# A blocked delta-rule kernel with a PReLU feed-forward: the first batch of 32-token blocks inverted to 16 tokens on VectorE and completed by 32x32 products on TensorE

## The chip, the cores and the metric

The kernel runs on one core of a Trainium2 chip. The metric is the device time of one execution in microseconds (us). Before the change, three runs took 712.58, 713.39 and 716.21 us; the median is 713.39 us.

## What is computed

There are two parts. The first is a delta rule over 4 batches x 8 heads, 768 tokens, 48 dimensions for each head. The second is a feed-forward block over the 3072 tokens (384 to 2048 to 384) with a learned slope for negative values. Cut to what matters:

```python
k_n = k / (norm(k) + 1e-6)
for t in range(S):                              # S = 768, state: 48 x 48 for each batch and head
    y[t] = q[t] @ state
    v_old = state.T @ k_n[t]
    state = state + beta[t] * outer(k_n[t], v[t] - v_old)
x = y as (3072, 384)
h = x @ w_in                                    # 384 x 2048, given as float64
g = maximum(h, 0) + alpha * minimum(h, 0)
out = g @ w_out                                 # 2048 x 384, given as float64
```

The recurrence is evaluated in chunks of 64 tokens. Within a chunk the updates depend on each other through a unit triangular 64x64 matrix made of the weighted products of the keys; the kernel needs its inverse.

## The kernel before

**Tiling.** One step is one chunk of 64 tokens of two batches (`t` = 0, 1 on partitions 0-63 and 64-127) and their 8 heads; there are N = 24 steps. Each 64x64 triangle is cut into two 32x32 diagonal blocks and the block between them (`right`). Four steps (NJ = 4) form a batch of blocks: 4 steps x 8 heads x 4 quadrants of 32 partitions, so that after a transpose VectorE holds one 32x32 block on each partition, as 128 x (32 x 32) elements (`block`).

**Inversion of the blocks.** `grams` (L372) makes the products of the keys on TensorE and puts the weighted diagonal blocks in `same` and the ones between in `right`. `turn_in` (L437) turns `same` into `block` by four transposes. `eliminate` (L444) masks the block, sets its diagonal to one, and does 30 steps `j`, each of one product and one sum over j x (31 - j) elements (L456, L462), each needing the one before. Then it writes the inverses back in both orientations, `turned` and `inverse`, by four transposes each. It yields after each piece: `WHOLE` = 31 + 8 = 39 pieces.

**The chain of a step.** `placing` (L486) copies parts of `turned` and `inverse` on ScalarE to `diag` and `inv`. Part 0 is the left block of `diag`, part 1 the right one, part 2 the blocks of `inv` and two small copies of weights. `between_1` and `between_2` (L524, L539) make the 32x32 block between the two diagonal ones of the inverse by two sets of 16 products each; `solve`, `outputs`, `next_state`, `to_ffn` follow. `scale_v` (L556) scales the values with the norms of the keys; `grams(N, n)` gives the products of queries and keys, masked by four VectorE instructions for each two steps (L396).

**The weights.** They arrive as 64-bit floats, 512 KB pieces of `w_in` and 384 KB pieces of `w_out`. Each piece costs two ScalarE instructions (`begin`, L204 and L205) and three on VectorE (`finish`, L212, L216, L220), the latter in two parts separated by a `yield`. Staging space holds six pieces of `w_in`; a finished piece lets SP fetch the next one into its place.

**Order of the work.** [...] that order is written by hand. `weave` takes parts from several generators in proportion to their lengths. The stages that matter here are these:

1. `statics(0, NJ - 1)`: keys of the first four steps, up to the batch of blocks 0.
2. `busy(BUSY)` with BUSY = 34: 34 products of 128x512 on TensorE whose result nobody reads, then `begin_in(n_in)` (six pieces) on ScalarE and `eliminate(0)` on VectorE.
3. The first chunk, steps 0 and 1: `ready(0, True, 1)` and `pair(0, 1)`, woven with 8 parts of `conv_in`. They carry seven more `busy(1)` products.
4. A weave of steps 2 and 3, 26 parts of conversion, `statics(4, 7)` and `ffn_in(0)`, the first product of the feed-forward for chunk 0.
5. A weave of the last conversion parts, `ffn_in(1)`, two more `statics` steps and the first 12 pieces of `eliminate(1)` (SOON = 12).
6. `ffn_out(0, True)` (64 records of L750) woven with the other 27 pieces of `eliminate(1)`. After that the regular loop over the steps 4 to 23 begins.

PSUM space: `ps_big` rotates through three buffers of two banks, `ps_ffn` through two of one bank; `busy` uses the latter.

Of the kernel before, what the change touches and what calls it, by code (L numbers as in the profile page):

```python
# [25 lines left out]
FP32 = mybir.dt.float32  # L26
# [6 lines left out]
C = 64  # L33
HB = 32
W_IN_P = 512
BUSY = 34
EARLY = 8
FIRST = 6

# [2 lines left out]
def kernel(  # L42
# [82 lines left out]
    def load_q(n):  # L125
        if n < N:
            fetch(q, n, q_pad[n % NQ][:, :, 0:D])
# [122 lines left out]
        out=ones, in_=ones, compare_op=ALU.is_ge, fill=1.0, base=0,  # L250
        pattern=[[1, HB], [-1, HB]], channel_multiplier=0,
    )
    inside = const.tile([128, HB, HB], S8, name="inside")

    which = const.tile([128, 2], FP32, name="which")
    nc.gpsimd.memset(which, 0.0)
    for t in range(2):
        for i in range(2):
            nc.gpsimd.memset(which[64 * t + HB * i : 64 * t + HB * (i + 1), i : i + 1], 1.0)


    beta_t = const.tile([128, NCH, NB, H], FP32, name="beta_t")
# [141 lines left out]

    NJ = 4
    same, block, inverse, turned = {}, {}, {}, {}

    def gather(n):
        m, j = n // NJ, n % NJ
# [25 lines left out]
            yield  # L435

    def turn_in(m):  # L437
        block[m] = work.tile([128, HB, HB], FP32, name="block", bufs=1)
        yield from turns(
            lambda x: block[m][:, :, x].rearrange("b r c -> b c r"),  # L440
            lambda x: same[m][:, :, :, x].rearrange("r j h c -> r c (j h)"),
        )

    def eliminate(m):  # L444

        if m > 2:
            yield from turn_in(m)
        r = block[m]
        nc.vector.tensor_tensor(out=r, in0=r, in1=inside, op=ALU.mult)
        nc.vector.memset(r.rearrange("p r c -> p (r c)")[:, :: HB + 1], 1.0)  # L450
        yield
        for j in range(1, HB - 1):
            n = HB - 1 - j
            prod = work.tile([128, HB * HB // 4], FP32, name="prod", bufs=2)
            prod = prod[:, 0 : j * n].rearrange("p (c i) -> p c i", c=j)
            nc.vector.tensor_tensor(  # L456
                out=prod,
                in0=r[:, 0:j, j : j + 1].to_broadcast([128, j, n]),
                in1=r[:, j : j + 1, j + 1 : HB].to_broadcast([128, j, n]),
                op=ALU.mult,  # L460
            )
# [3 lines left out]
            yield  # L465
        turned[m] = work.tile([128, NJ * H, HB], FP32, name="turned", bufs=1)
# [9 lines left out]
    WHOLE = HB - 1 + 2 * PIECES  # L476

    def changes(n):

        return n > NJ  # L480

    def place(n, parts=(0, 1, 2)):
        for _ in placing(n, parts):
            pass

    def placing(n, parts):  # L486


        if n >= N:
            return  # L490
        m, j = n // NJ, n % NJ
        first, second = slice(0, HB), slice(HB, C)

        def put(dst, cols, src, i, rows=slice(0, 128), to=None, a=slice(0, 2)):
            heads = slice(j * H + a.start * G, j * H + a.stop * G)
            nc.scalar.mul(
                dst[n % NE][to or rows, a.start * G : a.stop * G, cols], src[m][rows, heads],
                which[rows, i : i + 1],
            )

        if 0 in parts:
            put(diag, first, turned, 0)
            yield
        if 1 in parts:
            put(diag, second, inverse, 1, a=slice(0, 1 if changes(n) else 2))
            yield
            if changes(n):
                for t in range(2):
                    put(diag, second, inverse, 1, half(t), half(1 - t), slice(1, 2))
                    yield  # L510
        if 2 in parts:
            put(inv, first, inverse, 0)
            yield
            if changes(n):
                put(inv, second, inverse, 1)
                yield
            w = stats[n][1]
# [123 lines left out]
    sums = const.tile([128, FP, 3, 128], FP32, name="sums")  # L641
    more = const.tile([128, FP // 2, 3, DM // 2], FP32, name="more")
    FAST = 2

    def act_of(c, i):
        if c != 1:
# [226 lines left out]
    def busy(n):  # L873

        if n > 0:
            p = ps_ffn()
            for _ in range(n):
                nc.tensor.matmul(p, ident, k_t[NJ - 1].rearrange("p g i -> p (g i)"))  # L878

    def pair(n, filler=0):  # L880

        both = (n, n + 1)
        for i in both:
            through_state(i)
        yield
        for i in both:
            solve(i)
            busy(filler)
            yield
        for i in both:  # L890
            outputs(i)
            next_state(i)
            load_late(i + 2)
            load_v(i + 3)
            busy(filler)
            yield
        for i in both:
            to_ffn(i)
        yield

    READY = 5

    def ready(n, turned=False, filler=0):

        both = (n, n + 1)
        for i in both:
            place(i, (0,))
            if not turned:
                flips(N, i)
                load_q(i + 2)  # L910
        yield
        for i in both:
            between_1(i)
        busy(filler)
        yield
        for x in (1, 2):
            for i in both:
                place(i, (x,))
        for i in both:
            grams(N, i)  # L920
        yield
        for i in both:
            between_2(i)
            scale_v(i)
            busy(filler)
            yield

    def statics(first, last):
        if first > 0:
# [38 lines left out]
    def chain(*gens):  # L968
        for g in gens:
            yield from g  # L970
# [12 lines left out]
    for _ in statics(0, NJ - 1):  # L983
        pass
    nc.scalar.copy(inside, ones)
    load_late(1)
    load_v(2)
    for i in range(2):
        scale_v(i)

    slopes()
    for i in range(2):
        flips(N, i)
    for i in range(2):
        load_q(i + 2)
    nc.scalar.mul(minus, above, -1.0)
    zeros()

    busy(BUSY)
    begin_in(n_in)  # L1000
    for _ in eliminate(0):
        pass
    n = 8
    weave(
        (chain(ready(0, True, 1), pair(0, 1)), READY + PAIR), (part(conv_in, n), n)
    )
# [49 lines left out]
    tail = feed_forward()  # L1056
    for n in range(NJ, N):

        gens = [(attention(n), SHARES), (placing(n + 1, (1, 2)), SHARES * PLACING)]
# [51 lines left out]
```

## Time and profile before

| what | value |
|---|---|
| median of three runs | 713.39 us |
| profiled execution, its own time | 714.12 us |
| its span, first to last instruction | 712.3 us |
| mean granted TensorE clock | 0.994 |
| TensorE busy | 683.1 us (96%) |
| VectorE busy | 476.5 us (67%) |
| ScalarE busy | 251.2 us (35%) |
| GpSimd busy | 18.5 us (3%) |
| read from and written to memory | 31.56 MB, 4.72 MB |

The profile is of one execution. Times in it are counted from the first instruction. PE is TensorE's matmul, PEld its weight load, DVE VectorE, ACT ScalarE, POOL GpSimd, SP the engine that issues most transfers. A matmul on 32-bit floats appears as two records. `x64` behind a group is its number of records. Busy time includes the time for which a product that nobody reads runs.

### The profile page before, as it was taken

The numbers are of one execution on the slowest core, as the hardware profiler recorded it, in microseconds if no ns is written. First come the engines' busy times: TensorE is split into PE (matmuls) and PEld (weight loads), VectorE is DVE, ScalarE is ACT, GpSimd is POOL, SyncE is SP. The second block draws the span as 40 slices with busy tenths as digits, with TensorE's granted clock in tenths as the row PEclk, the third lists the DMA queues.
The fourth block names the chain that finished last, engine by engine and source line by source line (L and its number), as shares of the span: only waits on it lengthen the run. The fifth ranks groups of instructions, "written<-read, shape, count | busy, mean of one in ns | idle before, by whom it ended". The sixth has DMA issues, their size and how long they took to land.

```text
span 712.3 us, 21783 instructions
## 1 busy us (share of the span) xinstructions
PE 683.1 (96%) x9473; PEld 580.0 (81%) x9473; DVE 476.5 (67%) x1173; ACT 251.2 (35%) x596; POOL 18.5 (3%) x72
## 2 busy tenths in 40 slices
PE   5999987889999999999999999999999999999997
PEld 5457765656668898998998998898998988989997
DVE  6976889886898738868638968538967436245151
ACT  4724766433544413423433333222234124031020
POOL 3000000000000000000000000000000000000000
PEclk9999999999999999999999999999999999999999
DMA  8904944411141130130131021021111101100000
GB/s 135 227 30 99 220 140 99 130 23 34 35 81 25 35 68 13 36 66 16 34 68 36 6 54 35 8 51 35 25 35 35 35 24 35 24 12 2 23 1 22
DMA packets 110958, 37.68 MB, mean 53 GB/s; under 512 B 104160, under 2 KB 107248, under 8 KB 110864
## 3 DMA queue, kind: packets, MB, share of 16 engines
q1 hardware_dynamic: 109280, 36.01, 23.4%
q8 instruction: 74, 1.21, 0.7%
q10 hardware_dynamic: 1584, 0.30, 0.2%
q14 instruction: 20, 0.16, 0.1%
HBM read 31.56 MB, written 4.72 MB: 51 GB/s over the span
## 4 chain that ended last, share of the span: by engine, by line
PE 81%; DVE 12%; ACT 5%; issue 1%; DMA 1%; SPq 0%; DVEq 0%
PE p_ffn L709 29%; PE p_ffn L772 26%; PE p_ffn L878 5%; PE p_ffn L750 4%; PE p_big L378 3%; PE p_big L573 3%; PE p_big L345 3%; PE p_big L600 2%; PE p_big L587 2%; PE p_big L530 2%; PE p_big L545 1%; PE p_big L616 1%; DVE prod L456 1%; DVE block L462 1%; DVE act L721 1%
## 5 line engine op out<-in xcount | busy, mean ns | idle before, releaser
L709 PE MATMUL p_ffn<-xt,w_in 128*128 128x256 f32 x1152 | 269.7, 387 | 9.5 <-DVE sums L721 3.2
L709 PEld LDWEIGHTS p_ffn<-xt,w_in 128*128 128x128 f32 x1152 | 213.9, 191 | 42.8 <-ACT w_out L204 6.8
L721 DVE SCALAR_TENSOR_TENSOR act<-act,al_t,p_ffn 128x256 f32<-128x256 f32 x176 | 76.4, 476 | 72.3 <-ACT act L719 71.4
L719 ACT ACTIVATE act<-p_ffn 128x512 f32<-128x512 f32 x88 | 52.3, 594 | 117.1 <-PE p_ffn L709 116.9
L772 PE MATMUL p_ffn<-w_out,act 128*128 128x192 f32 x480 | 83.7, 328 | 0.0
L772 PEld LDWEIGHTS p_ffn<-w_out,act 128*128 128x128 f32 x480 | 78.6, 190 | 0.9
L462 DVE TENSOR_TENSOR block<-block,prod 128x30 f32<-128x30 f32 (+9 forms) x180 | 59.7, 332 | 6.2
L456 DVE TENSOR_TENSOR prod<-block 128x30 f32<-128x30 f32 (+9 forms) x180 | 58.7, 326 | 3.3
L792 DVE TENSOR_TENSOR o_sb<-u,p_ffn 128x192 f32<-128x192 f32 x40 | 13.2, 351 | 42.4 <-PE p_ffn L772 36.1
L878 PE MATMUL p_ffn<-k_t,ident 128*128 128x512 f32 x82 | 38.8, 622 | 0.0
L581 ACT COPY y<-p_big 128x384 f32<-128x384 f32 x22 | 10.5, 478 | 67.9 <-DVE r L576 67.9
L367 ACT COPY q_t<-p_big 128x512 f32<-128x512 f32 x24 | 14.0, 588 | 57.4 <-PE p_big L345 57.4
L367 ACT COPY k_t<-p_big 128x512 f32<-128x512 f32 x24 | 13.9, 580 | 55.6 <-PE p_big L345 55.5
L422 ACT COPY same<-right 32x256 f32<-32x256 f32 x40 | 16.1, 403 | 48.6 <-DVE right L387 48.3
L878 PEld LDWEIGHTS p_ffn<-k_t,ident 128*128 128x128 f32 x82 | 15.6, 199 | 17.1 <-issue 16.7
L772 PE MATMUL p_ffn<-space_out,sums 128*128 128x192 f32 x160 | 29.3, 326 | 0.0
L772 PE MATMUL p_ffn<-more,sums 128*128 128x192 f32 x160 | 29.3, 326 | 0.0
L772 PE MATMUL p_ffn<-w_out,sums 128*128 128x192 f32 x160 | 27.7, 326 | 0.0
L772 PEld LDWEIGHTS p_ffn<-space_out,sums 128*128 128x128 f32 x160 | 26.5, 190 | 0.0
L772 PEld LDWEIGHTS p_ffn<-more,sums 128*128 128x128 f32 x160 | 26.5, 190 | 0.0
L792 DVE TENSOR_TENSOR u<-u,p_ffn 128x192 f32<-128x192 f32 x20 | 7.0, 352 | 28.9 <-PE p_ffn L772 28.7
L772 PEld LDWEIGHTS p_ffn<-w_out,sums 128*128 128x128 f32 x160 | 25.8, 190 | 0.0
(131 smaller groups left out, 952.7 us busy)
## 6 DMA issues: line engine op xcount, KB each, us to landing
w_out<-in_moe_w_in_dram SPq DMA_DIRECT2D x12, 512.0 KB, 5.3
qp<-in_q_dram SPq DMA_DIRECT2D x48, 96.0 KB, 2.9
v_raw<-in_v_dram SPq DMA_DIRECT2D x48, 96.0 KB, 2.9
kl<-in_k_dram SPq DMA_DIRECT2D x96, 48.0 KB, 2.4
out_dram<-o_sb SPq DMA_DIRECT2D x96, 48.0 KB, 1.6
space_out<-in_moe_w_out_dram SPq DMA_DIRECT2D x11, 384.0 KB, 4.2
ke<-in_k_dram SPq DMA_DIRECT2D x43, 96.0 KB, 3.6
w_out<-in_moe_w_out_dram SPq DMA_DIRECT2D x5, 384.0 KB, 3.0
```

The lines of the kernel that those rows point to most:

```text
L345: nc.tensor.transpose(p[:, g * 128 : (g + 1) * 128], src[:, 2 * g : 2 * g + 2].rearrange("p h d -> p (h d)"), ident,)
L367: nc.scalar.copy(dst.rearrange("p g i -> p (g i)"), src)
L378: nc.tensor.matmul(p[half(t ^ a if w else t), a, w, g], k_t[n][dims(a), g, half(t)], rhs[n][dims(a), g, half(t)],)
L456: nc.vector.tensor_tensor(out=prod, in0=r[:, 0:j, j : j + 1].to_broadcast([128, j, n]), in1=r[:, j : j + 1, j + 1 : HB].to_broadcast([128, ...
L462: nc.vector.tensor_tensor(out=r[:, 0:j, j + 1 : HB], in0=r[:, 0:j, j + 1 : HB], in1=prod, op=ALU.add)
L573: nc.tensor.matmul(p[half(t), a, w, g], x[n][dims(a), g, half(t)], state[bp][dims(a), t, g])
L709: nc.tensor.matmul(p_h[:, i], w_in[:, t, (f + i) * 128 : (f + i + 1) * 128], xt[:, t], start=(t == 0), stop=(t == KT - 1),)
L719: nc.scalar.activation(g, p_h, ACT.Relu, scale=-1.0)
L721: nc.vector.scalar_tensor_tensor(out=g[:, i], in0=g[:, i], scalar=al_t[:, f + i : f + i + 1], in1=p_h[:, i], op0=ALU.mult, op1=ALU.add,)
L750: nc.tensor.matmul(p_o[u], gs[f // 2][:, f % 2, u * 128 : (u + 1) * 128], w_out[:, f], start=(f == 0), stop=(f == FT - 1),)
L772: nc.tensor.matmul(p, x(i), w(i), start=(i == 0), stop=(i == FP - 1))
L878: nc.tensor.matmul(p, ident, k_t[NJ - 1].rearrange("p g i -> p (g i)"))
```

## The change

**Blocks.** `block` gets 32 spare elements at its end, so that one view (`own_blocks`) can address the two 16x16 diagonal blocks inside each 32x32 block. For the first batch, `eliminate_small` masks these two, sets the rest of the block to zero by two memsets and the diagonal to one, and does 14 steps over both at once, each over 2 x j x (15 - j) elements. `back`, the transposes at the end, is taken out of `eliminate` and shared. The other batches are inverted as before.

**The 16x16 blocks between.** `edges` copies the part of `same` that lies between the 16-token blocks to `edge` on ScalarE, with the rows of the other half set to zero by `first_of` (a new constant, one VectorE reduction). `cross` then completes `turned` and `inverse` for a range of blocks: 4 products of 32x32 by 32x16 for each block, a ScalarE copy to `half_way`, 2 and 4 more for each block, and three VectorE sums. It is called for the 16 blocks of steps 0 and 1 in `first_chunk`, and for the 16 blocks of steps 2 and 3 at the head of the next weave. `edge` lies in `sums` and `half_way` in `act`, which are free at that time; two GpSimd memsets clear parts of them.

**First chunk.** `ready(0, ...)` and `pair(0, ...)` woven with conversion are replaced by `first_chunk`, whose order is written out, with 6 parts of conversion instead of 8 and five `busy(1)` instead of seven. The products of queries and keys of steps 0 and 1 (`queries`) are issued ahead of `busy(BUSY)`, their masks within `first_chunk`; `scale_v` of steps 0 and 1 moves from before the elimination into `first_chunk`. The small copies of weights become part 3 of `placing` and are issued ahead for steps 0 and 1.

**Numbers.** BUSY goes from 34 to 8, `begin_in` from six pieces to four, SOON from 12 to 8.

```diff
-BUSY = 34
+BUSY = 8
...
-    inside = const.tile([128, HB, HB], S8, name="inside")
+    inside_ = const.tile([128, HB * (HB + 1)], S8, name="inside")
+    inside = inside_[:, 0 : HB * HB].rearrange("p (r c) -> p r c", c=HB)
...
+    first_of = const.tile([128, 1], FP32, name="first_of")
+    nc.vector.tensor_reduce(
+        out=first_of, in_=ident.rearrange("p (q u e) -> p u q e", u=2, e=HB // 2)[:, 0],
+        axis=mybir.AxisListType.XY, op=ALU.add,
+    )
...
+    def eliminate_small(m):
+        x = small[m]
+        nc.vector.tensor_tensor(out=x, in0=x, in1=own_blocks(inside_), op=ALU.mult)
+        nc.vector.memset(block[m][:, 0:LB, LB:HB], 0.0)
+        nc.vector.memset(block[m][:, LB:HB, 0:LB], 0.0)
+        nc.vector.memset(block[m].rearrange("p r c -> p (r c)")[:, :: HB + 1], 1.0)
+        yield
+        for j in range(1, LB - 1):
+            n = LB - 1 - j
+            prod = work.tile([128, HB * HB // 4], FP32, name="prod", bufs=2)
+            prod = prod[:, 0 : 2 * j * n].rearrange("p (s c i) -> p s c i", s=2, c=j)
+            nc.vector.tensor_tensor(
+                out=prod,
+                in0=x[:, :, 0:j, j : j + 1].to_broadcast([128, 2, j, n]),
+                in1=x[:, :, j : j + 1, j + 1 : LB].to_broadcast([128, 2, j, n]),
+                op=ALU.mult,
+            )
+            nc.vector.tensor_tensor(
+                out=x[:, :, 0:j, j + 1 : LB], in0=x[:, :, 0:j, j + 1 : LB], in1=prod, op=ALU.add
+            )
+            yield
+        yield from back(m)
+
+    def edges(m, dst):
+
+        src = same[m].rearrange("p j h c -> p (j h) c")[:, :, LB:HB]
+        nc.scalar.mul(dst[:, :, LB:HB], src, first_of)
...
+    def cross(m, bs, edge, half_way):
+
+        n = bs.stop - bs.start
+        p = ps_one()[:, 0 : n * LB].rearrange("p (b i) -> p b i", i=LB)
+        for b in range(n):
+            for i in range(4):
+                nc.tensor.matmul(
+                    p[quad(i), b], edge[quad(i), bs.start + b],
+                    turned[m][quad(i), bs.start + b, 0:LB],
+                )
+        nc.scalar.copy(half_way[:, bs, 0:LB], p)
+        yield
+        p = ps_big()[:, :, 0 : n * LB].rearrange("p w (b i) -> p w b i", i=LB)
+        for b in range(n):
+            for i in (0, 2):
+                nc.tensor.matmul(
+                    p[quad(i), 1, b], inverse[m][quad(i), bs.start + b],
+                    half_way[quad(i), bs.start + b, 0:LB],
+                )
+        for b in range(n):
+            for i in range(4):
+                nc.tensor.matmul(
+                    p[quad(i), 0, b], half_way[quad(i), bs.start + b],
+                    inverse[m][quad(i), bs.start + b, LB:HB],
+                )
+        for i in (0, 2):
+            y = turned[m][quad(i), bs, 0:LB]
+            nc.vector.tensor_tensor(out=y, in0=y, in1=p[quad(i), 1], op=ALU.add)
+        y = inverse[m][:, bs, LB:HB]
+        nc.vector.tensor_tensor(out=y, in0=y, in1=p[:, 0], op=ALU.add)
+        yield
...
+    edge, half_way = edge_space(sums, 0), edge_space(act, 3072)
+    nc.gpsimd.memset(edge[:, :, 0:LB], 0.0)
+    nc.gpsimd.memset(half_way[:, :, LB:HB], 0.0)
...
+    def first_chunk(mask, convert):
+
+        both = (0, 1)
+        middle = cross(0, slice(0, 2 * H), edge, half_way)
+        next(middle)
+        busy(1)
+        for i in both:
+            mask(i)
+        next(middle)
+        busy(1)
+        for i in both:
+            place(i, (0,))
+            scale_v(i)
+        for i in both:
+            between_1(i)
+            place(i, (1,))
+        convert(1)
+        busy(1)
+        for i in both:
+            place(i, (2,))
+            between_2(i)
+        for i in both:
+            through_state(i)
+        solve(0)
+        convert(1)
+        solve(1)
+        busy(1)
+        for i in both:
+            outputs(i)
+            next_state(i)
+            convert(1)
+            load_late(i + 2)
+            load_v(i + 3)
+        busy(1)
+        for i in both:
+            to_ffn(i)
+        convert(2)
...
     nc.scalar.copy(inside, ones)
+    edges(0, edge)
     load_late(1)
     load_v(2)
-    for i in range(2):
-        scale_v(i)
-
     slopes()
     for i in range(2):
         flips(N, i)
     for i in range(2):
         load_q(i + 2)
+    mask = queries()
     nc.scalar.mul(minus, above, -1.0)
     zeros()
+    for i in range(2):
+        place(i, (3,))
 
     busy(BUSY)
-    begin_in(n_in)
-    for _ in eliminate(0):
+    begin_in(4)
+    for _ in eliminate_small(0):
         pass
-    n = 8
-    weave(
-        (chain(ready(0, True, 1), pair(0, 1)), READY + PAIR), (part(conv_in, n), n)
-    )
+    n = 6
...
+    first_chunk(mask, convert)
     fetch_out(SPACES)
     n = PARTS_IN - n + 10
     weave(
-        (chain(ready(2), pair(2)), READY + PAIR), (chain(conv_in, part(conv_out, 10)), n),
+        (chain(cross(0, slice(2 * H, 4 * H), edge, half_way), ready(2), pair(2)),
+         CROSS + READY + PAIR),
+        (chain(conv_in, part(conv_out, 10)), n),
         (statics(NJ, 2 * NJ - 1), 2 * NJ + 1), (ffn_in(0), IN_PARTS),
     )
     fetch_out(len(stages))
-    blocks, SOON = eliminate(1), 12
+    blocks, SOON = eliminate(1), 8
```

More of the change, by code (lines that the diff above doesn't have):

```diff
@@ L406, with own_blocks @@
     same, block, inverse, turned = {}, {}, {}, {}
+    small = {}
+    LB = HB // 2
+    def own_blocks(flat):
+        x = flat.rearrange("p (s e) -> p s e", s=2)[:, :, 0 : HB * LB]
+        return x.rearrange("p s (r c) -> p s r c", c=HB)[:, :, :, 0:LB]
     def gather(n):
@@ L437, in turn_in @@
     def turn_in(m):
-        block[m] = work.tile([128, HB, HB], FP32, name="block", bufs=1)
+        flat = work.tile([128, HB * (HB + 1)], FP32, name="block", bufs=1)
+        block[m] = flat[:, 0 : HB * HB].rearrange("p (r c) -> p r c", c=HB)
+        small[m] = own_blocks(flat)
         yield from turns(
@@ L465, in eliminate, with back @@
             yield
+        yield from back(m)
+    def back(m):
+        r = block[m]
         turned[m] = work.tile([128, NJ * H, HB], FP32, name="turned", bufs=1)
@@ L476 @@
     WHOLE = HB - 1 + 2 * PIECES
+    def eliminate_small(m):
[19 more added lines that the diff above has]
+            yield
+        yield from back(m)
@@ new lines, in edges, with quad @@
+    def edges(m, dst):
+        src = same[m].rearrange("p j h c -> p (j h) c")[:, :, LB:HB]
+        nc.scalar.mul(dst[:, :, LB:HB], src, first_of)
+    def quad(i):
+        return slice(HB * i, HB * i + HB)
+    def cross(m, bs, edge, half_way):
[28 more added lines that the diff above has]
+        yield
@@ L478, in changes, with place @@
+    CROSS = 2
     def changes(n):
         return n > NJ
-    def place(n, parts=(0, 1, 2)):
+    def place(n, parts=(0, 1, 2, 3)):
         for _ in placing(n, parts):
@@ L516, in placing @@
                 yield
+        if 3 in parts:
             w = stats[n][1]
@@ L643, with edge_space @@
     FAST = 2
+    def edge_space(x, first):
+        flat = x.rearrange("p i s e -> p (i s e)")[:, first : first + NJ * H * HB]
+        return flat.rearrange("p (b i) -> p b i", i=HB)
+    edge, half_way = edge_space(sums, 0), edge_space(act, 3072)
+    nc.gpsimd.memset(edge[:, :, 0:LB], 0.0)
+    nc.gpsimd.memset(half_way[:, :, LB:HB], 0.0)
     def act_of(c, i):
@@ L878, in busy, with pair @@
                 nc.tensor.matmul(p, ident, k_t[NJ - 1].rearrange("p g i -> p (g i)"))
-    def pair(n, filler=0):
+    def pair(n):
         both = (n, n + 1)
@@ L887, in pair @@
             solve(i)
-            busy(filler)
             yield
@@ L894, in pair @@
             load_v(i + 3)
-            busy(filler)
             yield
@@ L901, with ready @@
     READY = 5
-    def ready(n, turned=False, filler=0):
+    def ready(n):
         both = (n, n + 1)
@@ L907, in ready @@
             place(i, (0,))
-            if not turned:
-                flips(N, i)
-                load_q(i + 2)
+            flips(N, i)
+            load_q(i + 2)
         yield
@@ L913, in ready @@
             between_1(i)
-        busy(filler)
         yield
-        for x in (1, 2):
+        for x in (1, 2, 3):
             for i in both:
@@ L924, in ready, with queries, mask @@
             scale_v(i)
-            busy(filler)
             yield
+    def queries():
+        p = ps_big().rearrange("p a (n g i) -> p a n g i", n=2, g=G)
+        for n in range(2):
+            for g, a, t in quarters():
+                nc.tensor.matmul(
+                    p[half(t ^ a), a, n, g], k_t[n][dims(a), g, half(t)],
+                    q_t[n][dims(a), g, half(t)],
+                )
+            a_t[n] = work.tile([128, H, C], FP32, name="a_t")
+        def mask(n):
+            for a in range(2):
+                nc.vector.tensor_tensor(
+                    out=a_t[n][:, a * G : (a + 1) * G], in0=p[:, a, n],
+                    in1=minus[:, None, :].to_broadcast([128, G, C]), op=ALU.mult,
+                )
+        return mask
+    def first_chunk(mask, convert):
[34 more added lines that the diff above has]
+        convert(2)
     def statics(first, last):
@@ L995, with convert @@
         load_q(i + 2)
+    mask = queries()
     nc.scalar.mul(minus, above, -1.0)
     zeros()
+    for i in range(2):
+        place(i, (3,))
     busy(BUSY)
-    begin_in(n_in)
-    for _ in eliminate(0):
-        pass
-    n = 8
-    weave(
-        (chain(ready(0, True, 1), pair(0, 1)), READY + PAIR), (part(conv_in, n), n)
-    )
+    begin_in(4)
+    for _ in eliminate_small(0):
+        pass
+    n = 6
+    def convert(n):
+        for _ in part(conv_in, n):
+            pass
+    first_chunk(mask, convert)
     fetch_out(SPACES)
@@ L1057 @@
     for n in range(NJ, N):
-        gens = [(attention(n), SHARES), (placing(n + 1, (1, 2)), SHARES * PLACING)]
+        gens = [(attention(n), SHARES), (placing(n + 1, (1, 2, 3)), SHARES * PLACING)]
         if n % NJ == 0 and n < N - NJ:
```

## The prediction

> **What bounds the kernel now.** I read the page first, then the busy time by stage, the chain of waits, and the instructions in order of time on VectorE and TensorE.
>
> ```profile
> span 712.3 us, 21783 instructions
> PE 683.1 (96%) x9473; PEld 580.0 (81%) x9473; DVE 476.5 (67%) x1173; ACT 251.2 (35%) x596; POOL 18.5 (3%) x72
> ```
>
> TensorE looks like the bound of everything. By stage it is not:
>
> ```profile
> 18.31:49.00 30.69, 30.69 (x71) 13.19 (x71) 27.69 (x76) 14.00 (x32) 0.00 (x0) 1.00 0.52 125
> 49.00:65.30 16.30, 16.30 (x405) 10.88 (x406) 9.47 (x20) 4.32 (x13) 0.00 (x0) 1.00 0.39 110
> 65.30:115.00 49.70, 45.15 (x784) 36.27 (x782) 40.03 (x91) 35.40 (x80) 2.36 (x8) 0.97 0.67 165
> 115.00:149.30 34.30, 25.22 (x167) 19.48 (x166) 30.86 (x84) 19.37 (x41) 2.25 (x4) 0.95 0.30 81
> 149.30:171.00 21.70, 21.65 (x100) 12.99 (x101) 18.27 (x50) 2.28 (x7) 0.60 (x2) 1.00 0.12 23
> ```
>
> Columns: stretch, length, busy PE, PEld, DVE, ACT, POOL, clock, DMA share, GB/s. In the first stretch TensorE is full, with 71 instructions. The chain says with what:
>
> ```profile
> 18.31 30.69 PE p_ffn L878 x68
> 49.00 1.99 PE p_big L530 x64
> 50.98 1.05 PE p_ffn L878 x2
> ```
>
> L878 is `busy`, products nobody reads. The useful work there is VectorE's elimination:
>
> ```profile
> 18.33 0.98 DVE L559 TENSOR_TENSOR v_raw<-v_raw,norm 128x384 f32<-128x384 f32 x2
> 19.23 1.22 DVE L449 TENSOR_TENSOR block<-block,inside 128x1024 f32<-128x1024 f32 x1
> 30.62 0.41 DVE L456 TENSOR_TENSOR prod<-block 128x240 f32<-128x240 f32 x1
> 31.50 0.41 DVE L456 TENSOR_TENSOR prod<-block 128x240 f32<-128x240 f32 x1
> 42.01 0.20 DVE L456 TENSOR_TENSOR prod<-block 128x30 f32<-128x30 f32 x1
> 42.50 1.96 DVE L434 STREAM_TRANSPOSE turned<-block 128x256 f32<-128x256 f32 x4
> 44.32 2.19 DVE L434 STREAM_TRANSPOSE inverse<-block 128x256 f32<-128x256 f32 x4
> ```
>
> It ends at 46.5, 2.5 us before the fillers let L530 start. From 18.3 to 49.0 no feed-forward work is possible; from 115 to 149 VectorE leads (90% busy); from 149 on TensorE does, with real work. So what is saved before 65.3 reaches the end, less what the middle stages take back.
>
> **What the Trainium skill says.** "TensorE: Matmul & The Clock Gate", section "What's actually happening": the array runs at half clock until a window of about 3.4 us was busy, and falls back after an idle one. The trace agrees: records of L878 begin 0.853 us apart at first, 0.429 us after about 3 us. The same page, "LDWEIGHTS (loading the stationary operand)": a load's time goes with the columns, about P/1.2 ns. "TensorEngine Tiling (Array Packing)", section "Key Properties": different tiles work in parallel. The trace agrees, by these rows:
>
> ```profile
> 48.93 2.06 PE L530 MATMUL p_big<-diag,right 64*64 64x32 f32 x64
> 51.97 1.16 PE L378 MATMUL p_big<-q_t,k_t 48*64 48x64 f32 x64
> 12.10 1.99 PE L378 MATMUL p_big<-k_t 48*64 48x64 f32 x64
> ```
>
> Each is 32 matmuls. L530 uses two tiles of the array: 62 ns for a matmul. L378 uses four: 34 ns. The third row is the second before the clock rises: 62 ns. No product of 32x32 by 32x16 is in the trace.
>
> **The elimination.** A pair L456 + L462 takes 0.88 us at 240 elements (30.62 to 31.50) and 0.49 at 30 (42.01 to 42.50): 0.43 + 0.0019 for an element. The old 30 pairs (4960 elements): 22.3 us, in the trace 22.0. The new 14 pairs hold 2 x j x (15 - j), 1120 in sum: 14 x 0.43 + 2.1 = 8.2 us. The mask covers 512 elements in place of 1024: 0.75 (half of 1.3, and a fixed part). The two memsets of 256 are not shown: between 0.1 (L450, 32 elements, 0.09) and 0.35 (an L462 of that size, 0.43) each; I take 0.25. `scale_v` no longer stands ahead, so the start is 18.3, not 19.2. Sum: 18.3 + 0.75 + 0.5 + 0.05 + 8.2 = 27.8; `turned` at 29.7, `inverse` at 31.8 (the transposes as before, 1.82 to the second set, then 2.19). The old `turned` came at 44.5.
>
> Ahead of this, at no cost: the reduction `first_of` runs while VectorE waits 4.0 us for the first keys; the POOL memsets (two of 512 elements, at most 0.95 each by the 1024 of L248) fill its 1.7 us idle ahead of L334 at 8.0 (0.2 us late at most); `edges` (about 0.6) lies in ScalarE's 2.7 us wait ahead of L284; part 3 (0.8) and four `begin` pieces (5.1, by L204 and L205) end near 30, before `half_way` needs ScalarE. `queries` takes 2 us at low clock after the q flips at 18.3, then eight fillers, about two slow, end near 28. SP's loads keep their order; those of `load_late` and `load_v` come 15 us sooner, behind transfers that ended at 33.
>
> **The products.** For 16 blocks: 64 on four tiles, then 32 on two, 64 on four. At the rows above 2.2 + 2.0 + 2.2 = 6.4 us, the upper bound. These weights have 32 columns, not 64; if the load sets the pace it is half, 3.2, the lower bound (not under nothing, it is added). I take 1.6 + 3.1 = 4.7.
>
> **The first chunk.** TensorE from `turned` on: 1.6; filler 0.86; 3.1; filler 0.86; L530 2.0; filler; L545 2.1; L587 1.2; filler; L600 and L616 2.2; filler; L629 0.66: 17.2, and about 0.4 of waits. ScalarE and VectorE fit beside it: `half_way` (0.4), masks (1.4) and sums (0.35 each) beside fillers and products; `scale_v` (0.98) sits behind the last sum and ahead of the `inv` sum, three fillers' time before solve; the conversions in front of u (0.7) and the state (1.1) delay the second u behind a filler. If that cover fails it costs about 1. So the weave begins at 29.7 + 17.6 = 47.3 instead of 65.3: **-18.0**.
>
> **The next weave.** It takes the other 16 blocks: TensorE 4.7, VectorE 1.1, ScalarE 0.4. One more piece of `w_in` on VectorE (0.4 + 0.7 + 0.7 = 1.8) and two on ScalarE (2.6). TensorE is busy 91% there, VectorE 81, ScalarE 71, each often awaiting another: **+4.0** (2 to 6.5).
>
> **SOON.** Four pieces of elimination (j = 8 to 11) leave the stage in which VectorE leads: -2.8 (4 x 0.69, from 137.83 to 147.87). In the next, VectorE ended at 168.7 and TensorE at 169.6; it now ends 3.2 later, 2.3 behind. What waits is `placing` of step 4 and its `between_2`; TensorE has L750 of the next chunk meanwhile. Some +1.3. Together **-1.5** (-3 to +0.5).
>
> **The clock.** Between the fillers' end near 28 and the first filler of the chunk near 31.3 TensorE does little: 1.7 us of nothing, 1.6 us of quarter-array products. A window there may count as idle; then one window of 3.4 us runs at half speed: **+1.7** (0 to 15). From 49 to 65 the mix of fillers and small products stayed at full clock; from 5 to 13 small products and transposes alone never raised it.
>
> **Sum.** -18.0 + 4.0 - 1.5 + 1.7 = -13.8. The profiled execution took 714.1: 700.3. The median shown lies 0.7 below it: **699.6**, I say 700 us.
>
> **Rivals.**
> *The clock stays low through the chunk* (0.14). For: the stretch 5 to 13, and that the fillers fall from 34 to 8 and from seven to five. Against: the stretch 49 to 65, where one window held only a quarter filler. Half the chain slow costs 8.6 instead of 1.7: 707. All of it: 715.
> *The middle gives it back* (0.11): the weights don't come sooner or the three engines wait for each other more. For: the DMA share there is 0.67. Against: only 1.5 us of waits on transfers from 115 to 150, none of note earlier, and the DMA rests from 34 to 48. Stage +10 instead of +4: 706.
> *The small products don't run side by side* (0.09): slower than before. If row tiles that share a bank exclude each other, or each switch drains, a product takes what one tile needs, 2 x 62 = 124 ns: 160 of them 19.8 us instead of 4.7, in the chunk and again in the weave. 700 + 2 x 15.1 = 730. It decides from (713.4 - 700) / 320 = 42 ns above my 29, at 71 ns. Against: L530 runs two row tiles into one bank at 62, half of 124.
>
> **How the numbers follow.** The forecast has 0.66. Its own ends are 695 (products at the lower bound, -3; no slow window, -1.7) and 706. The range 695 to 709 takes in the first two rivals but for their tails and leaves out the third. This kernel's measurement can tell about 0.5% from no change: below 709.8 counts as faster, above 717.0 as slower. Faster: 0.66 + 0.10 + 0.10 = 0.86. Slower: 0.09. Same: 0.05.
>
> **What would show it.** In the profile after: the elimination's pairs end near 28; the products' group begins near 30 and takes about 1.6 and 3.1; the first L709 of the weave stands near 48 (66.6 before), the last `sums`/`more` L721 before L750 14 us sooner than 149.2, and VectorE's last transpose after TensorE's last L750 of that stage. I am wrong if L878 in the chunk shows 0.85 between its two records, if the products take over 10 us, or if the stage 65 to 115 has grown by more than 7.

## The result, and the profile after

The changed kernel takes 702.66 us in the median of four runs (699.69 to 703.72; a fifth on record took 703.84) beside 713.99 for the kernel before in the same session, now with a fourth run: a ratio of 0.9836, with a 95% interval from 0.9801 to 0.9872. The forecast was 700 us with a range from 695 to 709.

The profiled execution took 699.69 us, span 697.9. That is the quickest of the four, and the difference matters below. Its page begins:

```profile
span 697.9 us, 22933 instructions
PE 668.1 (96%) x10057; PEld 578.0 (83%) x10057; DVE 467.0 (67%) x1150; ACT 251.8 (36%) x599; POOL 19.4 (3%) x74
```

TensorE lost 15.0 us of busy time (683.1 before) in spite of 584 more records: what went is fillers. The busy time by stage, cut as before (columns: stretch, length, busy PE, PEld, DVE, ACT, POOL, granted clock, DMA share, GB/s):

```profile
18.15:48.50 30.35, 27.54 (x741) 18.22 (x742) 22.71 (x65) 16.30 (x42) 0.00 (x0) 1.00 0.60 151
48.50:101.20 52.70, 48.87 (x1103) 39.68 (x1102) 44.10 (x98) 37.99 (x85) 2.54 (x8) 0.97 0.70 174
101.20:135.00 33.80, 24.98 (x167) 19.79 (x167) 29.10 (x77) 18.92 (x41) 2.20 (x4) 0.94 0.33 90
135.00:158.30 23.30, 23.30 (x100) 13.90 (x101) 21.16 (x58) 2.42 (x7) 0.51 (x2) 0.93 0.09 18
```

The clock column is not to be trusted at the start. It reads 1.00 for the first stage, before and after, although the records of the first fillers begin 0.85 us or more apart and the later ones 0.43: the traces hold no change of the clock before 21 us in the one and 22 us in the other.

The elimination and the first chunk together took 47.0 us before (18.31 to 65.3) and take 30.4 now. On VectorE, in order of time:

```profile
18.87 0.69 DVE L502 TENSOR_TENSOR block<-block,inside 128x512 f32<-128x512 f32 x1
19.57 0.27 DVE L503 MEMSET block<- 128x256 f32 x1
23.65 0.27 DVE L517 TENSOR_TENSOR block<-block,prod 128x112 f32<-128x112 f32 x1
27.62 0.21 DVE L517 TENSOR_TENSOR block<-block,prod 128x28 f32<-128x28 f32 x1
27.86 1.99 DVE L448 STREAM_TRANSPOSE turned<-block 128x256 f32<-128x256 f32 x4
29.70 2.15 DVE L448 STREAM_TRANSPOSE inverse<-block 128x256 f32<-128x256 f32 x4
```

`turned` is complete at 29.85; before it was at 44.46. TensorE, in order of time, goes on from there:

```profile
29.10 1.40 PE L537 MATMUL p_big<-turned,sums 32*32 32x16 f32 x128 [0.96 <-DVE turned L448]
30.43 1.12 PE L975 MATMUL p_ffn<-k_t,ident 128*128 128x512 f32 x2
32.00 1.12 PE L546 MATMUL p_big<-act,inverse 32*32 32x16 f32 x61 [0.45 <-DVE inverse L448]
33.03 1.49 PE L552 MATMUL p_big<-inverse,act 32*32 32x16 f32 x124
34.46 1.12 PE L975 MATMUL p_ffn<-k_t,ident 128*128 128x512 f32 x2
36.03 2.37 PE L618 MATMUL p_big<-diag,right 64*64 64x32 f32 x64 [0.45 <-ACT diag L583]
39.39 2.00 PE L633 MATMUL p_big<-diag,mid 64*64 64x32 f32 x62
47.72 0.82 PE L717 MATMUL p_big<-ident,y 128*128 128x128 f32 x6
```

L537, L546 and L552 are the 32x32 products, L975 the fillers (L878 before), L618 and L633 `between_1` and `between_2`. After L717, at 48.5, the next weave begins (65.3 before). Later markers, by start: the transposes of the second batch of blocks, 97.06 (110.91 before); the long group of L847 (L750 before), 135.00 (149.35); its first product of the next chunk, 157.79 (170.63). So 16.8 us are gained by 48.5, 13.9 by 97.1, 14.4 by 135.0 and 12.8 by 157.8. The last 1.6 us up to the end come from single stretches near 272 and 447 us in which the profiled execution of the kernel before lost time over the same instructions; near 447 TensorE rests for 0.9 us of it.

### The profile page after: what moved, and what is told of

Read it like the earlier page. It is cut to its first block, busy times and chain, and to the rows that moved or that the text cites. A ratio compares the mean times of both kernels' runs of the same rounds, so it can differ in the third digit from the quotient of the medians.

```text
span 697.9 us, 22933 instructions
## 1 busy us (share of the span) xinstructions
PE 668.1 (96%) x10057; PEld 578.0 (83%) x10057; DVE 467.0 (67%) x1150; ACT 251.8 (36%) x599; POOL 19.4 (3%) x74
## 3 DMA queue, kind: packets, MB, share of 16 engines
q8 instruction: 79, 1.29, 0.8%
## 4 chain that ended last, share of the span: by engine, by line
PE 78%; DVE 13%; ACT 4%; issue 2%; SPq 2%; DMA 1%; DVEq 0%; ACTq 0%
PE p_ffn L806 30%; PE p_ffn L869 27%; PE p_ffn L847 4%; PE p_big L661 3%; PE p_big L352 2%; PE p_big L385 2%; PE p_big L688 2%; PE p_big L675 2%; PE p_big L618 2%; PE p_big L633 2%; PE p_big L704 1%; SPq L119 1%; DVE act L818 1%; DVE block L478 1%; DVE prod L472 1%
## 5 line engine op out<-in xcount | busy, mean ns | idle before, releaser
L478 DVE TENSOR_TENSOR block<-block,prod 128x30 f32<-128x30 f32 (+9 forms) x150 | 49.7, 332 | 5.2
L472 DVE TENSOR_TENSOR prod<-block 128x30 f32<-128x30 f32 (+9 forms) x150 | 48.7, 325 | 2.3
L374 ACT COPY k_t<-p_big 128x512 f32<-128x512 f32 x24 | 13.9, 580 | 55.3 <-PE p_big L352 55.2
L847 PE MATMUL p_ffn<-w_out,act 128*128 128x384 f32 x64 | 22.6, 515 | 3.4 <-DVE more L818 2.4
L583 ACT ACTIVATE diag<-inverse,which 64x128 f32<-64x128 f32 (+2 forms) x62 | 25.4, 412 | 0.9
```

The source lines that it names most:

```text
L472: nc.vector.tensor_tensor(out=prod, in0=r[:, 0:j, j : j + 1].to_broadcast([128, j, n]), in1=r[:, j : j + 1, j + 1 : HB].to_broadcast([128, ...
L478: nc.vector.tensor_tensor(out=r[:, 0:j, j + 1 : HB], in0=r[:, 0:j, j + 1 : HB], in1=prod, op=ALU.add)
L583: nc.scalar.mul(dst[n % NE][to or rows, a.start * G : a.stop * G, cols], src[m][rows, heads], which[rows, i : i + 1],)
L847: nc.tensor.matmul(p_o[u], gs[f // 2][:, f % 2, u * 128 : (u + 1) * 128], w_out[:, f], start=(f == 0), stop=(f == FT - 1),)
```

## The experiments

Each ratio, with its 95% interval in brackets, is to the kernel before in the same session; there it had medians of 713.12, 714.93, 713.96 and 713.31 us in the four sessions. The changed kernel itself was timed in two sessions alone, so most comparisons with it are across sessions. "The chunk" below is the time from the first `turned` transpose to the first product of the next weave.

**Are the parts worth what they were said to be?** Three runs take the change apart. The first undoes SOON.

```diff
-    blocks, SOON = eliminate(1), 8
+    blocks, SOON = eliminate(1), 12
```

> The changed kernel with SOON back at 12, so that four more steps of the second batch's elimination stand in the stage where VectorE leads. My forecast gave SOON 1.5 us of the gain: this run should then be 1 to 2 us slower than the changed kernel (about 704), with the long group of L847 starting some 2.5 us later relative to the start of that stage (36.3 us long instead of 33.8) and VectorE ending with TensorE in the next. Rival, that SOON is worth nothing because that stage waits on something else: the stage is as long as in the changed kernel, time within 0.5 us of it.

Measured: 702.67 us, 0.9824 (0.9766 to 0.9882), the changed kernel to 0.01 us. That is closer than the runs can tell: these four spread from 696.53 to 703.20, and the interval is 4 us to either side. The trace says more. In its profile the stretch from the second batch's transposes to the long group of L847 is 38.9 us instead of 38.0, and the long group is shorter (139.09 to 160.37, 21.3 us, instead of 22.8):

```profile
139.09 20.23 PE L847 MATMUL p_ffn<-w_out,act 128*128 128x384 f32 x62 [2.39 <-DVE more L818]
```

In the changed kernel that row reads 21.73. SOON moves about 1 us here, not 2.8, and what comes after varies by more. The 1.5 us are the clock: the group follows a rest of 2.4 us, and in 10 of the 14 profiles of this study it starts at half speed (stage of 22.8 to 23.0 us), in four not (21.3); both lengths occur with SOON 12 and with SOON 8.

Where SOON is 8 and the group is fast, the late end of VectorE that the prediction feared does show: in the two profiles of that kind (the one with BUSY 10 and the second one with a filler between the sets, both below) `between_2` behind the group waits 0.99 and 1.05 us for `mid`, and in this one, with SOON 12, not at all. So the two sides of SOON, about 1 us each, roughly cancel. That is nearer to the rival than to my 1.5 us, though the rival's equal length of the stage does not hold.

The second cuts four fillers from the kernel before.

```diff
-BUSY = 34
+BUSY = 30
```

> The kernel before with BUSY 30 instead of 34, so that the fillers end with the elimination instead of 2.5 to 3.5 us after it. If a part of the gain was only these fillers being too long, this gives it: four times 0.86, 3.4 us, so 710.5 (0.995). If the first product of the chunk was waiting for ScalarE or VectorE anyway, nothing: 714.

Measured: 709.64 us, 0.9951 (0.9933 to 0.9969). The 3.4 us come in full (3.5 in the medians): L530 starts at 45.74 instead of 48.93, at once behind the fillers. About a third of the change's gain could be had with this one number.

The third keeps the new order of the chunk and the whole 32-token elimination, without the products:

```diff
-BUSY = 8
+BUSY = 26
...
-    for _ in eliminate_small(0):
+    for _ in eliminate(0):
...
-        middle = cross(0, slice(0, 2 * H), edge, half_way)
-        next(middle)
-        busy(1)
         for i in both:
             mask(i)
-        next(middle)
-        busy(1)
...
-        (chain(cross(0, slice(2 * H, 4 * H), edge, half_way), ready(2), pair(2)),
-         CROSS + READY + PAIR),
+        (chain(ready(2), pair(2)), READY + PAIR),
```

> The new order of the first chunk, queries ahead, six parts of conversion, SOON 8, but the whole 32-token inversion by VectorE and none of the 32x32 products, with BUSY 26 so that the fillers end with it. My theory: the elimination makes most of the gain (14.8 us later blocks) and the order little; blocks ready near 44 instead of 29.1, no products (5.5 us less in the chunk, 3 less in the weave after): weave starts near 58, total about 705 to 708. Rival, that the order and the fillers are the gain: as fast as the changed kernel, about 700 to 702.

Measured: 705.37 us, 0.9886 (0.9856 to 0.9915). This is inside what the theory said, but the theory's reason, that the order gives little, falls: the order and the fillers give 7.8 us, of which some 3.5 are the too long fillers of the kernel before, as the second run shows. The short elimination with its products gives 2.7 more in the medians, and 2.0 beside the later session of the changed kernel; ten of the eleven executions of that kernel on record are under the fastest of these four (704.37). TensorE's rows in order of time show a short chunk:

```profile
45.25 2.06 PE L618 MATMUL p_big<-diag,right 64*64 64x32 f32 x64
48.29 2.00 PE L633 MATMUL p_big<-diag,mid 64*64 64x32 f32 x62
56.31 0.82 PE L717 MATMUL p_big<-ident,y 128*128 128x128 f32 x6
```

11.7 us from L618 to the weave, where the kernel before needed 16.4 (48.93 to 65.3): four fillers fewer, of about 1.06 us from start to start, and the query products (1.0) issued ahead. Between the two profiles the inversion should be worth more: 704.3 against 697.9 in span, 6.4 us. Why the medians give it only 2.7 was the next question.

**Why is the median 3 us above the profile?** The clock was the suspect, and the fillers in the chunk its handle.

```diff
     # in first_chunk, five times
-        busy(1)
+        busy(0)
```

> The changed kernel without the five single fillers in the first chunk. If they only take TensorE's time, the chunk is 2 to 4 us shorter and the total about 699 to 701. If they hold the clock up, the chunk's products show their slow distance (L618 4 us for both instead of 2), the chunk is up to 5 us longer and the total is 703 to 707.

Measured: 701.66 us, 0.9836 (0.9805 to 0.9867), no slower than with the fillers. Yet in its profile the small products are slow: L618 takes 3.6 us for both steps and L633 3.5. The chunk pays for a low clock and saves five fillers; at 21.8 us it is 1.2 longer than in the first profile of the changed kernel.

```profile
35.86 3.62 PE L618 MATMUL p_big<-diag,right 64*64 64x32 f32 x64 [1.48 <-ACT diag L583]
39.29 3.50 PE L633 MATMUL p_big<-diag,mid 64*64 64x32 f32 x62
```

Next, the fillers ahead were made to end later and, in another run, left out:

```diff
-BUSY = 8
+BUSY = 10
```

> The changed kernel with BUSY 10 instead of 8: the fillers end 1.7 us later, near 30, and the second set of 32x32 products starts when it did, since it waits for the inverse transposes until 31.9. My theory now: in most executions the clock falls in the chunk, because TensorE rests for a microsecond and then runs only small products, and that makes the difference between the profiled 699.7 and the median 702.7. With the gap closed the clock should hold: L618 and L633 at the fast distance (2 us for each pair of steps), a chunk of 20 to 21 us, median 700 to 701. Rival, that the spread comes from elsewhere: median 702.5 to 704, or later by the two fillers.

Measured: 704.15 us, 0.9848 (0.9820 to 0.9875), where the rival had it. The theory fails in one part: the gap is closed (the fillers end where L537 begins), and the clock falls all the same. That the time goes with the clock stands:

```profile
20.14 9.78 PE L975 MATMUL p_ffn<-k_t,ident 128*128 128x512 f32 x20
29.85 1.43 PE L537 MATMUL p_big<-turned,sums 32*32 32x16 f32 x128
31.21 1.12 PE L975 MATMUL p_ffn<-k_t,ident 128*128 128x512 f32 x2
35.62 2.03 PE L975 MATMUL p_ffn<-k_t,ident 128*128 128x512 f32 x2
37.59 3.63 PE L618 MATMUL p_big<-diag,right 64*64 64x32 f32 x64
```

The filler at 31.21 is fast, the one at 35.62 takes twice as long. In the 3.3 us between them TensorE issued small products, with one gap of 0.8 us. Together these didn't hold the clock; which of the two brings it down, this run doesn't tell.

```diff
-BUSY = 8
+BUSY = 0
```

> The changed kernel with BUSY 0, so that TensorE rests during the elimination. If the clock in the chunk depends on the fillers ahead, all of the chunk runs at half clock until the single fillers or the feed-forward raise it: L537 takes about 2.7 us instead of 1.4, the single fillers 2.1 instead of 1.1, the chunk 26 to 30 us, total 708 to 712. If the products and the single fillers raise the clock themselves within a window, the chunk is 22 to 24 us and the total about 703 to 705.

Measured: 705.36 us, 0.9875 (0.9850 to 0.9900). The chunk is as the first theory said, slow from the start (27.9 us against 20.6 in the first profile of the changed kernel), but the total is as the second said, only 2.7 us above the changed kernel: had the clock usually held there, this run would have lost about 7. That fits a changed kernel that is itself slow in most executions.

The changed kernel was then profiled once more, without an edit.

> The changed kernel once more, without an edit, for a second profile of it. My theory: its profile at 699.7 was of an execution in which the clock held, and most others, about 702.7, are slow in the chunk: L618 and L633 at 3.5 us for their pair instead of 2, the chunk 24 to 26 us instead of 20.5. Rival, that the other executions lose their 3 us elsewhere: the chunk is 20 to 21 us in this profile too while its time is over 702.

Measured: 703.42 us in the median of six, 0.9842 (0.9811 to 0.9874); the profiled execution took 704.43. Its TensorE rows in the chunk, to be read beside those of the first profile:

```profile
28.75 1.62 PE L537 MATMUL p_big<-turned,sums 32*32 32x16 f32 x128
30.30 1.12 PE L975 MATMUL p_ffn<-k_t,ident 128*128 128x512 f32 x2
34.95 2.08 PE L975 MATMUL p_ffn<-k_t,ident 128*128 128x512 f32 x2
36.96 3.63 PE L618 MATMUL p_big<-diag,right 64*64 64x32 f32 x64
42.52 3.52 PE L633 MATMUL p_big<-diag,mid 64*64 64x32 f32 x62
52.36 1.12 PE L975 MATMUL p_ffn<-k_t,ident 128*128 128x512 f32 x2
```

And the same stretch by busy time, first in the profile of 699.7, then in this one:

```profile
28.00:48.40 20.40, 17.59 (x657) 13.05 (x656) 13.92 (x30) 6.63 (x15) 0.00 (x0) 1.00 0.40 84
```

```profile
28.00:48.40 20.40, 19.53 (x521) 14.51 (x520) 9.70 (x23) 5.17 (x12) 0.00 (x0) 0.65 0.28 51
```

The granted clock is 1.00 there in one and 0.65 in the other: in the second it is at half speed from 34.0 to 51.0. The chunk is 27.0 us instead of 20.6; the two executions end 4.7 us apart, since later stages give 1.7 back. This is shown: one program, two courses, and the difference lies in the chunk. It also shows why a single profile misleads: the first was taken where the clock held.

What starts the fall is not settled. In each of the eight profiles in which the clock fell in the first chunk after full-speed fillers, the 3.4 us ahead of the fall held small products and also 0.7 to 2.4 us of rest. In the first profile, where it held, such a stretch with 0.7 us of rest had a whole filler in it. So neither the rests nor the smallness of the products is shown to be enough alone.

**Can it be held?** One more filler, between the two last sets of products:

```diff
     # in cross, for the first chunk
                     half_way[quad(i), bs.start + b, 0:LB],
                 )
+        busy(1)
         for b in range(n):
             for i in range(4):
```

> The changed kernel with one more single filler, between the two last sets of 32x32 products of the first chunk, so that no stretch of small products is longer than 2 us. If small products count as rest for the clock and the filler is enough to hold it: L618 and L633 fast, chunk 21 to 22 us, median 699 to 701, at least 1.5 us under the changed kernel in the same call. If the clock falls all the same, the filler costs 0.9 to 1.7 us and the median is 703 to 705.

Measured: 698.93 us, 0.9809 (0.9772 to 0.9845); the changed kernel in the same session 703.42. In the profile all is fast, the chunk 21.2 us:

```profile
32.21 1.12 PE L976 MATMUL p_ffn<-k_t,ident 128*128 128x512 f32 x2
33.27 1.61 PE L553 MATMUL p_big<-inverse,act 32*32 32x16 f32 x128
36.37 2.06 PE L619 MATMUL p_big<-diag,right 64*64 64x32 f32 x64 [0.44 <-ACT diag L584]
39.41 2.00 PE L634 MATMUL p_big<-diag,mid 64*64 64x32 f32 x62
```

> The version with one more filler between the two last sets of products, unchanged, a second time. If the filler holds the clock in most executions, at least four of six are under 701.5 us and the median is 698 to 701, clear of the changed kernel's 702.7 and 703.4. If the first time was luck, the median is 702 to 704.

Measured: 701.50 us, 0.9827 (0.9791 to 0.9863), between what the two theories said; three of six were under 701.5. Its profile is of an execution (704.06) in which the clock fell in the middle of the first filler:

```profile
29.60 1.59 PE L976 MATMUL p_ffn<-k_t,ident 128*128 128x512 f32 x2
33.04 2.08 PE L976 MATMUL p_ffn<-k_t,ident 128*128 128x512 f32 x2
38.88 3.63 PE L619 MATMUL p_big<-diag,right 64*64 64x32 f32 x64
```

Of all twelve executions of this version eight were under 701.3 us, of eleven of the changed kernel two. The limit was set after seeing the times. So the filler seems to make the good course likelier, and it doesn't make it sure. Whether the version is truly quicker than the changed kernel the intervals, which overlap, don't settle.

A longer variant, with the sum into `turned` between the sets, BUSY 9 and a filler ahead of `solve`:

```diff
-BUSY = 8
+BUSY = 9
...
+        busy(1)
         solve(0)
```

> The filler between the sets, the sum into turned issued between them, BUSY 9 and one more filler ahead of solve: the version with the best chance to hold the clock. If it holds: chunk 21.5 to 23 us with fast products, median 699.5 to 701. If not, slower than the changed kernel by the three fillers, 704 to 706.

Measured: 702.99 us, 0.9850 (0.9816 to 0.9884). In its profile (706.65) the clock fell again, here behind a wait of 1.0 us for `diag` inside L620. No gain from the two further fillers is to be seen.

The earlier sum by itself:

```diff
         for b in range(n):
             for i in (0, 2):
-                nc.tensor.matmul(p[quad(i), 1, b], inverse[m]..., half_way...)
+                nc.tensor.matmul(x[quad(i), b], inverse[m]..., half_way...)
+        for i in (0, 2):
+            y = turned[m][quad(i), bs, 0:LB]
+            nc.vector.tensor_tensor(out=y, in0=y, in1=x[quad(i)], op=ALU.add)
+        p = ps_one()[:, 0 : n * LB]...
         for b in range(n):
             for i in range(4):
```

> The changed kernel with the sum into turned issued between the two last sets of 32x32 products, each set in a PSUM buffer of its own. In the profile of the changed kernel the sum starts at 34.6, after all products, though its own ended at 33.1; diag then waits for it and L618 for diag (0.45 us). If that wait sets the chunk, the sum starts near 33.2, L618 right behind the filler at 35.5, and the chunk is 0.5 us shorter here and as much in the next weave: 0.5 to 1 us in all, within the noise of the time. If the turned sum doesn't come sooner, nothing changes.

Measured: 701.76 us, 0.9837 (0.9811 to 0.9864). The sum does come sooner: it starts at 34.75, behind its own set and 1.7 us before the other set ends. L618 (here L619) stands right behind the filler without a wait for `diag`, but the clock had fallen in the profiled execution and the filler took 2.1 us, so the gain can't be read there. The median is within the noise: inconclusive, as small as was said.

**What does a product cost?**

```diff
     # in cross, for each of the three sets
-        for b in range(n):
+        for b in [x for x in range(n) for _ in range(2)]:
```

> The changed kernel with every 32x32 product issued twice (the second overwrites the first with the same numbers). Each product took about 23 ns in the changed kernel (3.8 us for 160). If they are on the path with that price, the chunk is 3.8 us longer, and the weave after it 2.5 to 3.8: total 709 to 710. If waits beside them (the inverse transposes, ScalarE's diag) hide a part, the total is 705 to 708. If the products keep TensorE active enough to hold the clock, the chunk is not slow in this run in spite of them.

Measured: 728.28 us, 1.0197 (1.0169 to 1.0226). None of the theories: 25.6 us more than the changed kernel for 320 products more, 80 ns each, where the first set of 64 had taken 1.4 us, 22 ns each. TensorE in order of time:

```profile
28.94 2.70 PE L537 MATMUL p_big<-turned,sums 32*32 32x16 f32 x233 [0.68 <-DVE turned L448]
34.19 0.51 PE L537 MATMUL p_big<-turned,sums 32*32 32x16 f32 x23 [2.56 <-issue]
65.42 1.40 PE L537 MATMUL p_big<-turned,sums 32*32 32x16 f32 x128 [0.86 <-issue]
69.42 1.37 PE L537 MATMUL p_big<-turned,sums 32*32 32x16 f32 x107 [2.60 <-issue]
79.62 1.55 PE L552 MATMUL p_big<-inverse,act 32*32 32x16 f32 x128 [3.00 <-issue]
83.35 1.79 PE L552 MATMUL p_big<-inverse,act 32*32 32x16 f32 x119 [2.18 <-issue]
```

While the clock is up, the products themselves run at the same pace as in the changed kernel. Between them TensorE rests for 0.9 to 3.0 us with nothing that the profile shows to wait for ("issue"), and twice in these rows exactly 128 records lie between two such rests. With their weight loads these are 256 instructions. The seven rests of 0.4 to 3.0 us in this stretch come to 13.4 us, so they are only a part of the 25.6: the clock is at half speed from 32.5 to 59.8, and again from 70.0 to 73.4 and from 80.2 to 90.5.

The page's queue for instructions moved 1.29 MB in 79 packets for 22,933 instructions in the changed kernel, and 1.38 MB in 84 for 24,213 here: 1,280 more instructions, five more packets, 256 for each. The trace has the times of these packets, which come 3.4 to 8.7 us apart in this stretch. Each of the seven rests ends 1.3 to 1.6 us after one of them has come in. So TensorE very likely rests until its next packet of instructions is there; no run here took the packets away. The changed kernel has such rests too, in its chain of waits:

```profile
49.36 0.76 issue
54.19 0.76 issue
```

They end 1.6 and 1.5 us after a packet; of two shorter ones in its first chunk, one ends 1.4 and one 2.2 us after. In the second profile of the changed kernel the rest of 0.9 us among the products ahead of the fall of the clock ends 1.6 us after one.

## Why the prediction was right, and where it was not

By the profile of 704.43 us, which is like most executions (times from the first instruction, against the profile of before):

| step | forecast | measured, clock fell | measured, clock held |
|---|---|---|---|
| weave begins (65.3 before) | -18.0, clock apart | -11.2 | -16.8 |
| the next weave | +4.0 | +1.9 | +3.0 |
| SOON, both stages | -1.5 | +1.2 | +1.0 |
| the clock | +1.7 | in the first row | in the first row |
| the rest | 0 | -1.6 | -1.6 |
| sum | -13.8 | -9.7 | -14.4 |

The rows of the measured columns are differences of the markers named above. "Held" is said of the first chunk; in the next weave each of the two profiles has 3.4 us at half speed.

- *The elimination.* Right. The pairs ended at 27.86 (27.8 said), `turned` was ready at 29.85 (29.7). The memset of 256 took 0.27 us (0.25 taken). The match to 0.1 us is partly luck: the mask began at 18.87, not 18.3, and the pairs took 7.8 us, not 8.2.
- *The products.* Right in size for those issued: L537 1.4 us (1.6 said), L546 and L552 2.5 (3.1), nearly at the lower bound. Four row tiles of one bank took 22 ns for a product. A filler's 512 columns take 0.86 us at full clock, so 16 columns one product after another would be some 27 ns by estimate, without any weight load: the tiles did run side by side, as the Trainium skill, "TensorEngine Tiling (Array Packing)", section "Key Properties", says of different tiles. That the load sets the pace, the reason given for the lower bound, no run tests. In longer sets rests are added, as the doubled run shows.
- *The first chunk.* 48.5 in the profile where the clock held, 47.3 said. Two terms were too small. The waits came to 1.7 us where 0.4 was said: 0.45 for `inverse`, 0.45 for `diag` behind the sum into `turned`, which starts at 34.6, after all products, and not after its own, and 0.8 of "issue" in L675 and L688. The five fillers took 5.3 us where 4.3 was said: a single one between small sets costs about 1.06 from start to start, as the prediction's own row of the chain, 1.05 for L878, had it, and not 0.86. In exchange the products were 0.9 shorter, and L537 began at 29.10, with `turned` not yet complete.
- *The clock.* The mechanism was named and its place was right; its size was the step that failed. One slow window of 3.4 us, 1.7 us, was said, and 1 in 7 for half the chunk. In the second profile the clock stayed down from 34.0 to 51.0, and the chunk lost 6.4 us; of eleven executions of the changed kernel nine were near or above 702. The reason that failed was the comparison with the stretch 49 to 65 of the kernel before: there a filler stood between nearly any two sets, of larger tiles, and TensorE had no rests. Small products with rests among them are further from holding the clock than I took them to be, and once the clock was down it took 17 us, with three fillers among the sets, until it was up again.
- *The next weave.* +1.9 to +3.0 where +4.0 was said, at the lower end of its bounds (2 to 6.5).
- *SOON.* Failed in its size. VectorE was busy 90% of that stage and I took what leaves it as time gained. The stage gave about a third of that, 0.9 us of 2.8 beside the run with SOON 12. That the three engines wait for each other there is the likely reason, and not tested. The cost in the next stage was rightly named: 1.0 us of waiting at `between_2` shows in the two profiles with SOON 8 in which that stage is fast. In the profile above the stage is 1.5 us longer for another reason, the clock, and no such wait is left.

So the total was close because two errors stood against each other: the clock cost more than said, and in exchange the weave took less and the profile of before contained 1.6 us of its own. The rival that ended slower, products that don't run side by side, was excluded by L537. Its price of 71 ns for a product is passed when the products are doubled (80 ns), by rests and a low clock together, and not by what it named.

## What to carry to other kernels

A stage of dependent VectorE steps can be shortened by TensorE products, but count what holds the clock while they run: a row of small products with short rests in it can let the clock fall, and the loss of half the clock can last far longer than the products. Look at the granted clock in the stretch that was changed, over more than one profile, before believing the profile's total. And look first for fillers that are longer than what they cover: here one number gave a third of the gain.

## What the runs showed of the hardware

- TensorE's clock fell although it was never idle for long: in the run with ten fillers 3.3 us of 32x32 products (one gap of 0.8 us) lay between a fast filler and one at half speed. It also stayed low without any rest: in the second profile of the changed kernel TensorE is busy by its records for all of the 13.8 us from 34.0 to 47.8, with products on 32x32 and 64x64 tiles and two fillers, at half speed throughout. The Trainium skill, "TensorE: Matmul & The Clock Gate", section "What's actually happening", ties the fall to an idle window and the rise to a busy one. By these traces "idle" must take in windows with small products and short rests, and "busy" can't mean that the records leave no gap.
- The same section says that the window runs freely and gives about 3.4 us for it. The traces agree: of the half-speed stretches in the 14 profiles each lasts one to ten times 3.41 us, but for those that the end of the trace cuts off.
- Once it had fallen in the first chunk, the clock stayed low for 10.2 to 20.5 us, and for 27.3 when the products were doubled, with two to four single fillers of 2 us among the products where the chunk had them (from 34.0 to 51.0 in the second profile, with three). Without fillers in the chunk the time lay between, 13.7 us, to 47.5.
- Small products outrun something that feeds TensorE: when the products were doubled, it rested for 0.9 to 3.0 us under "issue" after 128 records. The rests end 1.3 to 1.6 us after a packet of the instruction queue, each packet standing for 256 instructions.
